# A Fourier layer and a soft mixture of experts on one core: which engine makes two low halves, one fused operation, and two places in the instruction order

## The chip, the cores and the metric

The kernel runs on one NeuronCore of a Trainium2 chip. The metric is the device time of one execution in microseconds, as a median of runs. The core's engines each work through an instruction list of their own in order: TensorE (PE in the profile, its weight loads PEld), VectorE (DVE), ScalarE (ACT), GpSimd (POOL) and SyncE (SP), whose queue issues nearly all DMAs.

## What is computed

The reference has two parts. The first takes x (8 x 2496 x 256), goes to frequencies along the sequence, applies a complex linear layer and a soft threshold, and goes back:

```python
X = np.fft.rfft(x, axis=1)
Yr = Xr @ w_r - Xi @ w_i + b_r
Yi = Xr @ w_i + Xi @ w_r + b_i
Yr = np.sign(Yr) * np.maximum(np.abs(Yr) - lam, 0.0)   # Yi the same
y = np.fft.irfft(Yr + 1j * Yi, n=x.shape[1], axis=1)
```

The second is a soft mixture of 8 experts with 4 slots each on the 19968 tokens of y:

```python
logits = y @ phi                                  # 19968 x 32
d = exp(logits - logits.max(0)); d /= d.sum(0)    # over the tokens
slot_input = d.T @ y                              # 32 x 256
slot_out[e] = relu(slot_input[e] @ w1[e]) @ w2[e]
c = exp(logits - logits.max(1)); c /= c.sum(1)    # over the slots
out = c @ slot_out
```

The inverse transform is linear, so the kernel never forms y: it carries phi, the weights d and the slots through the transforms.

## The kernel before

The 2496 points of a sequence are split as 39 x 64. A batch goes through three kinds of work.

**Steps.** There are 40 steps (`steps`), five per batch, each for four of the 20 frequencies of the 39-point transform. A step has the 64-point transform (`f2`, accumulators px, twice per step), the linear layer (`lin_k`, accumulator pk, 12 matmuls; `lin_y`, accumulators py, 24 matmuls in parts), the threshold (ut, rt), the product with phi (`tp_p`: matmuls pq, ScalarE's copy lg, a transposition of lg, VectorE's p_sb) and, for the last two steps of a batch, transpositions of rt (`tp_t`: accumulator pt, ScalarE's copy T). fp32 operands are split into a high half (rounded) and a low half (what is left), and a product is three matmuls: high, low part of the constant, low part of the operand. xsh and xsl, xh and xl, chpd and clpd are such pairs; xsl, xh and xl and the e = 0 rt are GpSimd's work.

**The 39-point transform** of later batches (`a_group`: xh, xl, accumulator pa, ScalarE's copies ast, written to DRAM and read back as ap).

**Stages of the mixture** (`c_stages`, once for each of batches 0 to 6; the last batch has a function of its own): logits in two transforms with a DRAM passage between (pg, gd, gp, then pL and its copies L), the maximum over the tokens (mx, transposition pm, mall as the running maximum over the batches), the exponentials of L less that maximum (dg, matmul pb, ee), their transforms with a second DRAM passage (pe, ea, ed, eb, then pd and its copies dd) and the sums over the tokens (pr). Beside it runs the softmax over the slots (`c_comb`: cm, cb, cs).

**The order.** Each of these pieces is a generator that yields a plan time; a heap takes the piece with the smallest time, and what it emits is put behind all earlier instructions of its engine. A step lasts 4 units of plan time, a batch 20. So the numbers of `PLAN` are an order written by hand: a number that passes another one moves an instruction in front of another on the same engine and does nothing else. `c_stages` of batch b counts from t0 = 20 b + 26, `tp_p` and `tp_t` of step s from 4 s + 6.

**What the change touches.** `halves` (L747) emits the split and the matmuls of pg, pL, pe and pd, for batches 0 to 5 (batch 6 has `fr` zero and no split). For each of two halves ScalarE copies the high half at `times[0] - 0.9 + 0.4 h`, and 0.3 later the engine that `cl_` names makes the low half (L759); the matmuls of half h come at `times[h]`, ScalarE's copy out of PSUM 0.25 later. For pd (`suni`) the letters are P for the first half and V for the second; the times are 18.1 and 19.05. `c_comb`'s last multiplication cb has the time 17.4 on the same scale. The second pL has 7.95, which is 20 b + 33.95; the px of a step stand at multiples of 4 and 2 units later, among them 20 b + 34. `tp_p` copies lg at 4 s + 7 and `tp_t` copies pt of h = 0 at 4 s + 6.92. L828 to L834 reduce the transposed maxima to `mall[:, b]`, take the maximum with `mall[:, b - 1]`, and scale the identity by it into dg.

Of the kernel before, what the change touches and what calls it, by code (L numbers as in the profile page):

```python
# [11 lines left out]
F32 = mybir.dt.float32  # L12
F32R = mybir.dt.float32r
AF = mybir.ActivationFunctionType
ALU = mybir.AluOpType
# [9 lines left out]
S = 32  # L25
# [54 lines left out]
def _constants():  # L80
# [93 lines left out]
    "sl": 'P',  # L174
    "c0": 0.05,
    "pg": [1.35, 2.3],
    "pL": [7.05, 7.95],
    "pm": 9.05,
    "pb": 10.32,
    "pe": [11.95, 12.98],  # L180
# [18 lines left out]
    "f0": 0.2,  # L199
    "nw": [13, 9],  # L200
    "te": 'A',
    "tp": [0.5, 1.0, 1.9, 1.8],
    "tt": [0.52, 2.505],
    "fr": {'sinv': 1, 'm2': 1, 'f1': 1, 'suni': 1},
    "cl": [0.9, 0.4, 0.3],
    "sc": [10.7, 13.18, 14.7, 17.306],
    "cl_": {'sinv': 'VV', 'm2': 'VV', 'f1': 'VV', 'suni': 'PV'},
    "pda": 1,
    "a1": [-50, -49, -28.95, -28.85, 3.0, 3.684, 6.147, 6.934, 8.231, 8.9, 9.713],
    "e1": [0, 0, 0, 0, 0, 0, 0, 0, 1, 0, 1],  # L210
# [45 lines left out]
def fourier_soft_moe_kernel(ctx: ExitStack, tc: tile.TileContext, t: dict, out: bass.AP):  # L256
# [21 lines left out]
    def wtile(shape, dt, tag, name):  # L278
        if tag in a_bufs:
            return wap.tile(list(shape), dt, tag=tag, name=name, bufs=a_bufs[tag])  # L280
        if tag in main_bufs:
            return wmp.tile(list(shape), dt, tag=tag, name=name, bufs=main_bufs[tag])
        return wcp.tile(list(shape), dt, tag=tag, name=name, bufs=chain_bufs[tag])
# [18 lines left out]
    V, A, P = (_InOrder(tc, e) for e in (nc.vector, nc.scalar, nc.gpsimd))  # L302
# [90 lines left out]
    ident, sgn, suni, sinv, dsc, dmask = (cols[k] for k in ("ident", "sgn", "suni", "sinv", "dsc", "dmask"))  # L393
    f1, m2 = cols["f1"][:P1], cols["m2"][:Q1]
# [11 lines left out]
    mall = cons.tile([128, B], F32, tag="mall", name="mall")  # L406
# [383 lines left out]
    def c_stages(b):  # L790
# [35 lines left out]
        )  # L826
        yield t0 + K_.get("pmr", K_["pm"] + 0.1)
        V.tensor_reduce(out=mall[:, b : b + 1], in_=ps[:, :P1], axis=AX.X, op=ALU.max)  # L828
        if b:
            V.tensor_tensor(  # L830
                out=mall[:, b : b + 1], in0=mall[:, b : b + 1], in1=mall[:, b - 1 : b], op=ALU.max
            )
        dg = wtile([128, S], F32, "dg", f"dg{b}")
        V.tensor_scalar(out=dg, in0=ident[:, :S], scalar1=mall[:, b : b + 1], scalar2=None, op0=ALU.mult)  # L834
        yield t0 + K_["pb"]
        ps = psum(ct_, f"pb{b}")
        mm(out=ps[:P1, :32], lhsT=ones, rhs=dg, start=True, stop=True)
# [3 lines left out]
            out=ee, in0=L[:P1], in1=ps[:P1, :32].unsqueeze(1).broadcast_to([P1, G, S]), op=ALU.subtract  # L841
        )
        if b:
            V.tensor_tensor(
                out=fo[:, b : b + 1], in0=mall[:, b - 1 : b], in1=mall[:, b : b + 1], op=ALU.subtract
# [335 lines left out]
    for b in range(B - 1):  # L1181
        step_to(c_stages(b))
# [248 lines left out]
    for j in range(NBLK):  # L1431
# [4 lines left out]
        for a in range(2):  # L1436
            mm(
                out=pq,
# [73 lines left out]
```

## Time and profile before

| | us |
|---|---|
| median of 3 runs | 552.43 (551.78 to 552.66) |
| the profiled execution | 554.82 |
| its span, first to last instruction | 552.9 |
| TensorE busy in the span | 500.0 (90%) |
| VectorE / ScalarE / GpSimd busy | 371.3 / 320.6 / 263.3 |
| mean granted TensorE clock | 0.954 |

The profile is one execution. A timeline row gives the start in us from the span's start, the duration, the engine, the line, the operation and the tiles as out<-in; a bracket at its end tells how long the engine was idle before it and what ended that. A start can lie some hundredths before the end of the instruction ahead of it on the same engine. Nearly all matmuls carry line 328 and the operations of the other engines line 252, since helpers record them, so the tiles' names tell them apart. The busy share of TensorE is no measure by itself; its waits and its clock say more.

### The profile page before, as it was taken

Reading aid. Unit: us, or ns where it says so; the run is one execution under the profiler, and the core shown is the slowest. Engines: PE = TensorE matmul, PEld = TensorE weight load, DVE = VectorE, ACT = ScalarE, POOL = GpSimd, SP = SyncE. Lnnn points to the kernel's source line nnn. Section 1 sums busy time; section 2 is a strip of 40 time slices with the busy share of each in tenths; the row PEclk is TensorE's granted clock in tenths of the full one; section 3 lists DMA queues with packets and bytes.
Section 4 is the critical chain, followed back from the end, with each engine's and each line's share of the span. In section 5 each row is a group of like instructions: output and inputs, shape, how many; then the busy total and the mean of one; then the engine's idle time right before and its main releaser. Section 6 shows DMA issues by size and latency. Waiting matters only on the chain.

```text
span 552.9 us, 11988 instructions
## 1 busy us (share of the span) xinstructions
PE 500.0 (90%) x4438; PEld 407.7 (74%) x4438; DVE 371.3 (67%) x718; ACT 320.6 (58%) x736; POOL 263.3 (48%) x277
## 2 busy tenths in 40 slices
PE   8879999997999979996999699969998999999991
PEld 5579778885787768785778678858887886558881
DVE  3347876788479836984688567865886477526771
ACT  4357567675566646673657466755565555427771
POOL 0028576667456655565565565662334432233310
PEclk9979999999799979997999799988998999999997
DMA  8988788688656866757485957673659799638998
GB/s 303 315 254 309 240 243 239 188 281 213 200 150 219 221 206 169 239 165 225 129 278 173 247 148 257 195 192 103 173 188 242 178 368 393 221 132 335 406 405 337
DMA packets 90461, 131.04 MB, mean 237 GB/s; under 512 B 40204, under 2 KB 61836, under 8 KB 90404
## 3 DMA queue, kind: packets, MB, share of 16 engines
q1 hardware_dynamic: 89460, 128.16, 72.5%
q10 hardware_dynamic: 944, 2.13, 1.2%
q8 instruction: 35, 0.57, 0.4%
q14 instruction: 22, 0.18, 0.1%
HBM read 69.25 MB, written 50.00 MB: 216 GB/s over the span
## 4 chain that ended last, share of the span: by engine, by line
PE 65%; DVE 10%; DMA 7%; POOL 7%; ACT 5%; issue 4%; SPq 1%; ACTq 0%; POOLq 0%; DVEq 0%
PE py L328 15%; PE pq L328 9%; PE pk L328 9%; PE pa L328 8%; PE px L328 8%; PE pt L703 3%; PE pr L328 3%; DVE mx L252 2%; POOL rt L252 2%; DMA gd<-g_sb 2%; PE pc L703 2%; PE pe L328 2%; DMA xr<-in_x 1%; PE pd L328 1%; POOL xsl L252 1%
## 5 line engine op out<-in xcount | busy, mean ns | idle before, releaser
L252 POOL TENSOR_TENSOR xsl<-xsm,xsh 128x256 fp32r<-128x256 f32 x77 | 65.5, 851 | 154.1 <-ACT xsh L252 139.5
L328 PEld LDWEIGHTS px<-smov,ap 128*128 128x128 f32 x640 | 79.5, 194 | 17.6 <-issue 5.7
L252 DVE SCALAR_TENSOR_TENSOR ut<-py,pk,k 128x256 f32<-128x256 f32 x160 | 69.8, 477 | 33.7 <-PE py L328 32.5
L328 PE MATMUL px<-smov,ap 128*128 128x128 f32 x640 | 86.9, 280 | 1.2 <-ACT ast L252 1.2
L252 DVE TENSOR_TENSOR xsm<-px,xsm 128x256 f32<-128x256 f32 x80 | 33.1, 414 | 57.9 <-ACT xth L252 28.1
L252 ACT COPY ast<-pa 128x512 f32<-128x512 f32 (+1 forms) x88 | 45.2, 558 | 27.9 <-PE pa L328 27.8
L252 DVE TENSOR_TENSOR xtl<-px,xth 128x512 fp32r<-128x512 f32 x80 | 54.3, 679 | 0.1
L328 PE MATMUL py<-xth,nwsh 128*128 128x256 f32 (+1 forms) x160 | 53.9, 337 | 0.0
L328 PE MATMUL pk<-xsh,w_rh 128*128 128x256 f32 (+1 forms) x160 | 50.6, 316 | 0.0
L252 ACT CAST xth<-px 128x512 fp32r<-128x512 f32 x80 | 47.1, 591 | 5.1 <-PE py L328 4.2
L252 POOL TENSOR_TENSOR rt<-ut,rt 128x512 f32<-128x512 f32 x36 | 50.0, 1389 | 0.1
L328 PE MATMUL pk<-xsl,w_rh 128*128 128x256 f32 (+1 forms) x160 | 48.2, 301 | 0.0
L328 PE MATMUL pk<-xsh,w_rl 128*128 128x256 f32 (+1 forms) x160 | 48.0, 300 | 0.0
L328 PE MATMUL py<-xth,wdh 128*128 128x256 f32 (+1 forms) x160 | 45.8, 286 | 0.0
L328 PE MATMUL py<-xtl,nwsh 128*128 128x256 f32 (+1 forms) x160 | 45.5, 284 | 0.0
L328 PE MATMUL py<-xth,nwsl 128*128 128x256 f32 (+1 forms) x160 | 45.4, 284 | 0.0
L328 PE MATMUL py<-xth,wdl 128*128 128x256 f32 (+1 forms) x160 | 45.3, 283 | 0.0
L328 PE MATMUL py<-xtl,wdh 128*128 128x256 f32 (+1 forms) x160 | 45.2, 283 | 0.0
L252 ACT COPY xsm<-px 128x256 f32<-128x256 f32 x80 | 30.0, 375 | 26.0 <-PE px L328 25.0
L252 POOL TENSOR_TENSOR xh<-xr 128x512 f32<-128x512 f32 (+1 forms) x36 | 44.2, 1227 | 0.0
L328 PE MATMUL pq<-rhs,ct 128*128 128x512 f32 x156 | 41.7, 405 | 0.2
L252 ACT CAST xsh<-xsm 128x256 fp32r<-128x256 f32 x80 | 33.1, 414 | 12.1 <-DVE xsm L252 11.7
(230 smaller groups left out, 1312.2 us busy)
## 6 DMA issues: line engine op xcount, KB each, us to landing
ap<-adr SPq DMA_DIRECT2D x76, 256.0 KB
out<-ost SPq DMA_DIRECT2D x37, 512.0 KB
xr<-in_x SPq DMA_DIRECT2D x35, 512.0 KB
adr<-ast SPq DMA_DIRECT2D x20, 768.0 KB
y<-z SPq DMA_DIRECT2D x112, 96.0 KB
w<-in_moe_w SPq DMA_DIRECT2D x21, 512.0 KB
adr<-ast SPq DMA_DIRECT2D x7, 512.0 KB
w<-in_moe_w SPq DMA_DIRECT2D x14, 256.0 KB
```

The lines of the kernel that those rows point to most:

```text
L252: return lambda *a, **k: self.tc.keep_in_program_order(f(*a, **k))
L328: tc.keep_in_program_order(nc.tensor.matmul(**kw))
L703: tc.keep_in_program_order(nc.tensor.transpose(out=out, in_=in_, identity=identity))
```

## The change

Four edits:

- `cl_`, `suni`: 'PV' becomes 'VP'. The first low half of pd's operand is made by VectorE, the second by GpSimd. It applies to batches 0 to 5.
- dg is made in one operation, (mall[b] max mall[b - 1]) times the identity, straight from the reduction; mall[b] itself gets the maximum behind it. Batches 0 to 6 (in batch 0 the second value is the first again).
- The second pL of batches 0 to 5 has the time 8.02 in place of 7.95, so that its matmuls stand behind the px at 34 + 20 b, and its copy and what follows it get 0.07 more.
- lg has the time 4 s + 6.9 in place of 4 s + 7: it stands ahead of the copy of pt at 4 s + 6.92.

```diff
@@ PLAN
-    "pL": [7.05, 7.95],
+    "pL": [7.05, 8.02],
-    "tp": [0.5, 1.0, 1.9, 1.8],
+    "tp": [0.5, 0.9, 1.9, 1.8],
-    "cl_": {'sinv': 'VV', 'm2': 'VV', 'f1': 'VV', 'suni': 'PV'},
+    "cl_": {'sinv': 'VV', 'm2': 'VV', 'f1': 'VV', 'suni': 'VP'},
@@ c_stages
         V.tensor_reduce(out=mall[:, b : b + 1], in_=ps[:, :P1], axis=AX.X, op=ALU.max)
+        dg = wtile([128, S], F32, "dg", f"dg{b}")
+        V.scalar_tensor_tensor(
+            out=dg, in0=mall[:, b : b + 1].broadcast_to([128, S]), scalar=mall[:, max(b - 1, 0) : max(b, 1)],
+            in1=ident[:, :S], op0=ALU.max, op1=ALU.mult,
+        )
         if b:
             V.tensor_tensor(
                 out=mall[:, b : b + 1], in0=mall[:, b : b + 1], in1=mall[:, b - 1 : b], op=ALU.max
             )
-        dg = wtile([128, S], F32, "dg", f"dg{b}")
-        V.tensor_scalar(out=dg, in0=ident[:, :S], scalar1=mall[:, b : b + 1], scalar2=None, op0=ALU.mult)
         yield t0 + K_["pb"]
```

## Rows read from the trace of the kernel before

**Rows 1.** The page, its chain that ended last, shares by engine.
```profile
PE 65%; DVE 10%; DMA 7%; POOL 7%; ACT 5%; issue 4%; SPq 1%; ACTq 0%; POOLq 0%; DVEq 0%
```
**Rows 2.** TensorE's waits: us in total, times, longest.
```profile
PE pd L328 <- POOL clpd L252: 24.2, 6, 4.4
PE pb L328 <- DVE dg L252: 5.6, 5, 1.2
PE pq L703 <- ACT lg L252: 2.5, 9, 0.7
```
**Rows 3.** Timeline around pd of batch 1, GpSimd and TensorE.
```profile
191.82 1.91 POOL L252 TENSOR_TENSOR rt<-ut,rt 128x512 f32<-128x512 f32 x1
...
194.62 1.26 POOL L252 TENSOR_TENSOR xl<-xr 128x512 f32<-128x512 f32 x1
195.84 0.85 POOL L252 TENSOR_TENSOR clpd<-eb,chpd 128x320 fp32r<-128x320 f32 x1
196.75 0.63 PE L328 MATMUL pd<-clpd,sunih 128*128 128x320 f32 x1 [4.43 <-POOL clpd L252]
```
**Rows 4.** Timeline of the same stretch, VectorE.
```profile
191.45 1.16 DVE L252 TENSOR_TENSOR cb<-cb,cs 128x704 f32<-128x704 f32 x1
192.53 1.55 DVE L252 TENSOR_TENSOR clpd<-eb,chpd 128x320 fp32r<-128x320 f32 x1
```
**Rows 5.** Timeline around pd of batch 5, VectorE and TensorE.
```profile
421.37 1.35 DVE L252 TENSOR_TENSOR clpd<-eb,chpd 128x320 fp32r<-128x320 f32 x1
...
423.49 0.42 PE L328 MATMUL pd<-clpd,sunih 128*128 128x320 f32 x1 [2.08 <-POOL clpd L252]
```
**Rows 6.** Stretches: length, busy of PE, PEld, DVE, ACT, POOL; clock, DMA, GB/s.
```profile
138.83:143.90 5.07, 5.07 (x23) 5.07 (x24) 1.96 (x4) 2.79 (x7) 0.73 (x1) 0.50 0.82 223
143.90:195.00 51.10, 47.08 (x463) 38.52 (x461) 39.97 (x75) 32.12 (x76) 31.68 (x32) 1.00 0.67 197
...
419.00:423.50 4.50, 2.06 (x15) 1.42 (x13) 3.50 (x6) 1.50 (x5) 3.67 (x3) 1.00 0.92 285
423.50:427.20 3.70, 3.70 (x18) 3.70 (x19) 1.62 (x3) 1.81 (x4) 0.73 (x1) 0.54 1.01 293
```
**Rows 7.** The chain that ended last, in order of time: start, us, what.
```profile
139.47 2.56 PE pk L328 x12
...
142.88 1.93 PE py L328 x12
...
151.75 0.89 PE px L328 x8
...
153.09 1.42 PE pk L328 x12
154.51 1.41 PE py L328 x12
```
**Rows 8.** By tile, clpg and dg: ns min/median/max, first and last start.
```profile
L252 DVE TENSOR_TENSOR clpg<-p_sb,chpg x12: 479/483/694, 93.2 to 381.9; 128x320 fp32r<-128x320 f32 x12
L252 DVE SCALAR_TENSOR_TENSOR dg<-mall,pk x1: 252/252/252, 469.0 to 469.0; 128x32 f32<-128x32 f32 x1
```
**Rows 9.** Timeline around dg of batch 1.
```profile
170.87 0.73 POOL L252 TENSOR_TENSOR xsl<-xsm,xsh 128x256 fp32r<-128x256 f32 x1 [1.97 <-PE pq L703]
171.17 0.45 DVE L252 TENSOR_TENSOR mall<-mall 128x1 f32<-128x1 f32 x1
171.56 1.26 POOL L252 TENSOR_TENSOR rt<-ut,rt 128x512 f32<-128x512 f32 x1
...
171.65 1.21 DVE L252 TENSOR_SCALAR dg<-pk,mall 128x32 f32<-128x32 f32 x1
...
172.78 0.86 DVE L252 SCALAR_TENSOR_TENSOR ut<-py,pk,k 128x256 f32<-128x256 f32 x2
172.91 0.39 PE L328 MATMUL pb<-dg,ones 128*117 128x32 f32 x2 [1.16 <-DVE dg L252]
...
176.44 0.53 DVE L252 TENSOR_TENSOR clpe<-ee,chpe 117x352 fp32r<-117x352 f32 x1 [0.21 <-ACT chpe L252]
```

## The prediction

> **What bounds the kernel now.** I read the page's chain first: of the work that ended last, TensorE is 65% [rows 1]. So the end moves only where TensorE waits or runs slowly, and the second view is the list of TensorE's waits [rows 2]. It is short: 24.2 us in six waits of the matmul group pd for its low half from GpSimd, 5.6 us in five waits of pb for dg, 2.5 us in nine waits of a transposition for lg. Each of these is touched by the change.
>
> The third view is the timeline around one pd, that of batch 1. TensorE's first pd group (high, low constant, low operand) stands still for 4.43 us until 196.75, so since 192.32 [rows 3]. What it waits for, GpSimd's clpd, runs at 195.84. It isn't late because its operand is: it stands in GpSimd's order behind rt, xh and xl, which ends only at 195.88 [rows 3]. VectorE made the other low half, of which pd needs only later, already from 192.53 on for 1.55 us [rows 4]. The wait is 4.43 us in batches 0 to 4 and 2.08 us in batch 5 [rows 2, 5].
>
> The fourth view is the granted clock. From 138.83, when the pd of batch 0 is released, to 143.90 it is 0.50, which is 1.2 GHz; from there to 195 it is 1.00, which is 2.4 GHz [rows 6]. So behind such a wait TensorE does its work at half speed: twelve pk matmuls take 2.56 us there and 1.42 us later, twelve py matmuls 1.93 and 1.41 [rows 7]. The 2.08 us wait of batch 5 has the same tail: 0.54 over 3.70 us [rows 6].
>
> **The change part by part. Low halves of pd.** The operation for the first half leaves GpSimd and goes to VectorE at plan time 17.5, that for the second goes to GpSimd at 17.9. On VectorE the multiplication cb (17.4) stands just ahead, p_sb behind. So the new operation stands where the old one stood in batch 1: directly behind cb, at 192.53 [rows 4]. What is it worth there? Alone, a subtraction of this size takes VectorE 0.483 us (clpg) [rows 8]; here it took 1.55 us. The rows say why: GpSimd's rt started at 191.82, while cb ran, took 1.91 us until 193.73, and the subtraction ended 0.35 us after it [rows 3, 4]. VectorE and GpSimd took turns: cb, rt, subtraction, in the order in which they came. I take the same end, 194.08, since neither the neighbours nor the place differ. TensorE then goes on at about 194.12 and waits 1.8 us in place of 4.43: 2.63 us less, five times, 13.1 us. In batch 5 VectorE's operation ran from 421.37 for 1.35 us, to 422.72, and pd was released at 423.49 [rows 5]: 0.7 us. Sum 13.9 us. The bounds: if VectorE gets no wait behind cb, the operation ends at 193.01 and the wait is 0.7 us, 3.7 us saved per batch; if it had to let xh and xl pass too, it would end 0.35 us behind 195.88, at 196.23, and 0.5 us is saved.
>
> The Trainium skill, "GPSIMD Engine Reference", section "4.1 Engine selection", would have such an operation on VectorE, since GpSimd is about twice as slow with two inputs. By that alone the first half would cost 0.48 us and the sum would be the upper bound, 19 us. The trace agrees when VectorE is alone (0.48 against 0.85 us) and not here, beside rt: 1.55 us [rows 3, 4, 8].
>
> What queues behind? On VectorE p_sb, which is needed only for the next pg, and after it work for a px that TensorE has only just made. On GpSimd the low half keeps its place behind xl and is for the second pd group. TensorE reaches that group after pk, transpositions and py: 194.12 plus 1.42 and 1.41 us is 196.95 [rows 7], and the transpositions come on top; GpSimd is done at 196.69 [rows 3]. So its wait is covered by 0.3 us and more; a longer GpSimd queue would show there.
>
> **The clock.** Per batch the half speed costs 1.14 us in pk and 0.52 in py [rows 7], 1.66 us; and since 5.07 us passed at half speed [rows 6] it can't be more than 2.5. I take 2.1, for the transpositions and the pd matmul between, five times 10.5. In batch 5 it is 3.70 times 0.46, 1.7 us [rows 6]. Together 12.2 us, if the clock doesn't fall. No row shows a wait of 1.8 us. Waits of 1.16 us left the clock at 1.00 (that of pb lies within the stretch from 143.90) [rows 6, 9]; one of 2.08 us didn't. So both ends, nothing and 12.2, are open. By distance 1.8 is nearer to 2.08; but the 2.08 us wait began at 421.41 and the stretch up to 423.5 still shows the clock at 1.00 [rows 6], so the fall came no sooner than some 2 us after the idling began, and a wait of 1.8 us is over by then, one of 1.35 all the more. I take the 12.2 us as regained and give the fall a large chance.
>
> **dg and the running maximum.** Removed from dg's path: the maximum (0.45 us) and the scaling (1.21 us); added: one operation that does both [rows 9]. In the last batch that very form took 0.252 us [rows 8]. It would be issued at 171.17, beside xsl, which GpSimd holds until 171.60, and be done by 171.75 instead of 172.86: pb's wait of 1.16 us goes. But what is next? The maximum itself now comes third, when rt (from 171.56, 1.26 us) already runs; dg took 1.21 us because it fell on rt, and the maximum will in its place [rows 9]. So VectorE's two ut begin no sooner than the 172.78 of today, rather 0.15 us later. py's accumulator is freed by them, and clpe (176.44), for which the third pe matmul would have to wait next, hangs on the VectorE chain behind them [rows 9]. TensorE gains 1.1 us at pb and gives it back at py and pe. I cost it at nothing; the bounds are 5.6 us gained [rows 2] and the 0.15 us lost per batch, 0.9 us.
>
> **Second pL behind px.** The matmuls stay, the eight px (0.89 us [rows 7]) go first. L's second copy comes up to 0.9 us later, which ScalarE's work on pa hides by half; with it the reduction mx, the head of the VectorE chain to dg. It takes from pb what dg's part gave. Between 0 and 0.45 us lost in each of six batches; I take 0.2, 1.2 us, since px and its ScalarE copies come earlier in exchange.
>
> **lg ahead of pt's copy.** It moves a copy that ScalarE could have made while it waited for pt. It removes the waits for lg where a pt stands beside: I take 1.1 of the 2.5 us [rows 2]; bounds 0 and 2.5. pt's copy isn't needed until pr, several us later. It also lets xsh and xsl start a little earlier; I count nothing for that.
>
> **Sum.** 13.9 + 12.2 + 0 - 1.2 + 1.1 = 26.0 us. The profiled execution took 554.82 us (span 552.9), 2.4 us over the median of 552.43; the differences hold for both, and I take them from the median: 526 us.
>
> **The rivals.** (1) The clock falls behind the shortened waits as well. For: 2.08 us was enough. Then 12.2 us of the sum is missing: 538 us, or some way between if it falls only in some batches (532 for half). Chance 0.25. (2) VectorE goes on straight behind cb and the operation takes 0.48 us: 5 times 1.1 us more, 520 us; against it speaks that the same two neighbours did take turns in batch 1. With dg's full 5.6 us it would be 515. Chance 0.10. (This is the case of the page named above.) (3) The change doesn't do what it says: VectorE's first half is held until GpSimd's queue is empty. Then five waits shrink by 0.5 us, 2.5 in all, the clock falls as before, and the time is about 550 us. Chance 0.03. (4) Slower: the VectorE chain from L's copy over mx, the held maximum and ut to ee and clpe becomes what TensorE waits for, 0.9 us of px plus 0.15 us in six batches, at most 6.3 us. It decides the sign once the pd part brings less than that, so only where the first half is held as in case 3: 552.4 - 2.5 + 6.3 is 556 us. Against it: none of these is a wait of TensorE's today. Chance 0.03. The forecast, 520 to 530 us by the bounds of the smaller parts, has the remaining 0.59.
>
> **Range and chances.** 516 to 539 us: from case 2 with half of dg's bound to the clock's full fall; it leaves out cases 3 and 4 and the far ends of the others. A measurement of this kernel can tell about 0.2% (1.1 us) from no change. Faster: 0.59 + 0.25 + 0.10, and a part of case 3, 0.95; same 0.02; slower 0.03.
>
> **What would show it.** In the profile after: pd's waits are for VectorE and some 1.8 us long, six in all, about 10 us; VectorE's clpd still takes 1.3 to 1.6 us; GpSimd's clpd ends before the second pd group; the granted clock is 1.00 right behind pd, and pk takes 1.4 us there; pb's waits are gone or small, and VectorE's maximum takes about 1.2 us in dg's place, with new waits of py for ut or of pe for clpe; waits for lg have halved. The prediction is wrong if the clock still falls behind pd, if the second pd group waits for GpSimd, or if a transfer (eb ahead of pd) is late once the batches are shorter.

## The result, and the profile after

The changed kernel takes 534.8 us (median of 4 runs, 533.44 to 537.2), the kernel before 552.28 us beside it (4 runs); the ratio is 0.969 with a 95% interval of 0.965 to 0.973. That is 17.5 us less, where 26 had been forecast: the time lies inside the range of 516 to 539 and 8.8 us above the predicted 526. The profiled execution took 533.44 us (span 531.7) beside the 554.82 (552.9) of before, and its mean granted clock is 0.972 where it was 0.954.

TensorE's waits after the change (us in total, times, longest), against [rows 2]:

```profile
PE pd L328 <- DVE clpd L252: 12.3, 6, 2.1
PE pb L328 <- DVE dg L252: 2.9, 6, 0.6
...
PE pe L328 <- ACT chpe L252: 1.0, 1, 1.0
PE py L328 <- DVE ut L252: 1.0, 5, 0.2
PE pq L703 <- ACT lg L252: 0.7, 1, 0.7
```

pd's six waits have halved, from 24.2 to 12.3 us, and VectorE now ends them instead of GpSimd. pb's went from 5.6 to 2.9 us, lg's from 2.5 to 0.7. Two small ones are new, py for ut and pe for chpe, 2.0 us together (before, pe waited for chpe for 0.2 us). Waits of pa early in the kernel differ from one execution to the next (for xr 0.4 us before and 2.0 after, for xh 2.1 before and none after) and are left aside here.

The timeline around pd of batch 1 answers to [rows 3, 4]:

```profile
183.83 0.88 DVE L252 SCALAR_TENSOR_TENSOR ut<-py,pk,k 128x256 f32<-128x256 f32 x2 [0.30 <-PE py L328]
184.62 1.00 DVE L252 TENSOR_TENSOR cb<-cb,cs 128x704 f32<-128x704 f32 x1
184.82 1.91 POOL L252 TENSOR_TENSOR rt<-ut,rt 128x512 f32<-128x512 f32 x1
185.54 1.54 DVE L252 TENSOR_TENSOR clpd<-eb,chpd 128x320 fp32r<-128x320 f32 x1
187.14 0.41 PE L328 MATMUL pd<-clpd,sunih 128*128 128x320 f32 x1 [2.05 <-DVE clpd L252]
188.88 0.87 POOL L252 TENSOR_TENSOR clpd<-eb,chpd 128x320 fp32r<-128x320 f32 x1
```

The order is the forecast one: cb, rt, subtraction. rt starts while cb runs and ends at 186.73; VectorE's subtraction, in line from 185.54, ends 0.35 us behind it, exactly the distance that [rows 3, 4] show. It takes 1.54 us, and TensorE waits 2.05 us, not 1.8. GpSimd's half ends at 189.75, and no second pd group waits for it.

The stretches around that pd (length, busy of PE, PEld, DVE, ACT, POOL; clock, DMA share, GB/s), against [rows 6]; the first is the one behind batch 0's pd, the second the wait itself:

```profile
134.20:140.00 5.80, 5.80 (x46) 4.80 (x47) 3.39 (x7) 4.24 (x10) 5.34 (x7) 1.00 0.88 248
185.08:187.14 2.06, 0.01 (x2) 0.01 (x1) 2.06 (x3) 0.00 (x0) 2.06 (x2) 1.00 0.90 304
187.14:187.58 0.44, 0.44 (x3) 0.44 (x4) 0.14 (x1) 0.00 (x0) 0.44 (x1) 1.00 0.94 214
187.58:190.99 3.41, 3.41 (x18) 3.41 (x17) 1.77 (x4) 1.92 (x5) 2.85 (x4) 0.50 1.01 291
```

Here the forecast's missing part is seen. Behind batch 0's wait the clock stays at 1.00, 2.4 GHz. Behind batch 1's it stays there for 0.44 us after TensorE has been released, and then falls to 0.50, 1.2 GHz, for 3.41 us. So it goes in five of the six batches, 0.44 to 0.66 us after the release. Before, it was at 0.50 for some 6.8 us around the end of each of the five long waits (it fell while they still ran, as in this stretch of batch 0's wait) and for 3.4 us behind batch 5's.

```profile
137.00:138.83 1.83, 0.00 (x0) 0.00 (x0) 0.00 (x0) 0.00 (x0) 1.78 (x2) 0.51 0.93 259
```

Around dg of batch 1, against [rows 9]:

```profile
164.52 0.72 POOL L252 TENSOR_TENSOR xsl<-xsm,xsh 128x256 fp32r<-128x256 f32 x1 [2.50 <-ACT xsh L252]
164.82 0.47 DVE L252 SCALAR_TENSOR_TENSOR dg<-mall,pk 128x32 f32<-128x32 f32 x1
165.20 1.27 POOL L252 TENSOR_TENSOR rt<-ut,rt 128x512 f32<-128x512 f32 x1
165.33 1.16 DVE L252 TENSOR_TENSOR mall<-mall 128x1 f32<-128x1 f32 x1
165.35 0.39 PE L328 MATMUL pb<-dg,ones 128*117 128x32 f32 x2 [0.49 <-DVE dg L252]
166.41 0.86 DVE L252 SCALAR_TENSOR_TENSOR ut<-py,pk,k 128x256 f32<-128x256 f32 x2
167.43 0.36 PE L328 MATMUL py<-xth,nwsh 128*128 128x256 f32 x1 [0.19 <-DVE ut L252]
```

dg ends at xsl's end and releases pb after 0.49 us. The maximum of one column, which pb does not need (the difference fo behind pb and the next batch's dg are the first to read it), now stands beside rt, takes 1.16 us and holds ut; py waits for ut in turn. The whole stall moved from dg to the maximum, as forecast.

### The profile page after: what moved, and what is told of

It is laid out like the page before. It is cut to its first block, busy times and chain, and to the rows that moved or that the text cites. A ratio compares the mean times of both kernels' runs of the same rounds, so it can differ in the third digit from the quotient of the medians.

```text
span 531.7 us, 11986 instructions
## 1 busy us (share of the span) xinstructions
PE 494.4 (93%) x4438; PEld 399.9 (75%) x4438; DVE 371.0 (70%) x718; ACT 321.1 (60%) x736; POOL 265.3 (50%) x277
## 5 line engine op out<-in xcount | busy, mean ns | idle before, releaser
L252 POOL TENSOR_TENSOR xsl<-xsm,xsh 128x256 fp32r<-128x256 f32 x77 | 66.9, 870 | 143.0 <-ACT xsh L252 142.6
L328 PEld LDWEIGHTS px<-smov,ap 128*128 128x128 f32 x640 | 78.3, 192 | 21.6 <-issue 7.6
L328 PE MATMUL pk<-xsh,w_rh 128*128 128x256 f32 (+1 forms) x160 | 49.0, 306 | 0.0
L328 PE MATMUL pk<-xsh,w_rl 128*128 128x256 f32 (+1 forms) x160 | 46.8, 292 | 0.0
```

Of the source, the lines that this page charges most:

```text
L252: return lambda *a, **k: self.tc.keep_in_program_order(f(*a, **k))
L328: tc.keep_in_program_order(nc.tensor.matmul(**kw))
```

## Experiments

What was open was twofold: whether the gain comes from the swapped halves at all, and whether the missing 9 us are the clock's falls or sizes of other terms. The runs come in three groups; those of one group share a chip and the runs of the kernel before, and each ratio is against those.

### The change again, and its parts

> The changed kernel as it is, beside the kernels of the next three runs on one chip. Every theory: 533 to 537 us, pd waits for VectorE some 2.05 us in six batches (12.3 us), and the clock falls behind most of them for 3.4 us.

The same kernel on another chip: 532.59 us (531.85 to 533.77) against 552.59, ratio 0.965 (0.961 to 0.969). The waits of pd are the same, 12.3 us in six, but the clock fell behind four of them. Three stretches (columns as above) show a fall that comes late, and none behind a wait of nearly the same length (2.00 us):

```profile
244.82:246.30 1.48, 1.48 (x12) 1.48 (x13) 0.14 (x1) 1.03 (x3) 1.48 (x2) 1.00 1.02 316
246.33:249.74 3.41, 3.41 (x18) 3.41 (x17) 2.45 (x4) 2.12 (x5) 2.37 (x4) 0.50 0.88 262
299.35:304.00 4.65, 4.65 (x40) 4.08 (x40) 3.06 (x7) 3.61 (x8) 4.19 (x5) 1.00 1.02 306
```

pd of batch 2 was released at 244.82; TensorE worked at full speed for 1.5 us, and only then the clock fell. Batch 3's wait (297.35 to 299.35) left it at 1.00, and so did the 2.05 us of batch 4. This execution also prices a fall by itself: from pb to pb a batch takes 54.55 us with one (168.46 to 223.02, 223.02 to 277.55) and 53.05 without (277.55 to 330.60), so a fall costs 1.5 us.

The swap alone, on the kernel before:

```diff
-    "cl_": {'sinv': 'VV', 'm2': 'VV', 'f1': 'VV', 'suni': 'PV'},
+    "cl_": {'sinv': 'VV', 'm2': 'VV', 'f1': 'VV', 'suni': 'VP'},
```

> The kernel before with one edit alone: the first low half of pd's operand by VectorE, the second by GpSimd. Theory A (the gain is pd's shorter wait and the shorter fall of the clock behind it): pd waits about 1.8 us per batch, 1.35 in batch 5, and the time is 535 to 539 us, over three quarters of the gain. Rival B (the four edits only work together; alone the swap brings half or less): 543 us or more.

535.26 us (535.02 to 535.84), ratio 0.970 (0.966 to 0.974): nearly all of the gain. Its waits, the timeline of batch 1, and the stretches of pd's wait and behind it:

```profile
PE pd L328 <- DVE clpd L252: 10.9, 6, 1.8
PE pb L328 <- DVE dg L252: 5.8, 5, 1.2
```

```profile
185.19 0.88 DVE L252 SCALAR_TENSOR_TENSOR ut<-py,pk,k 128x256 f32<-128x256 f32 x2 [0.22 <-PE py L328]
...
186.36 1.91 POOL L252 TENSOR_TENSOR rt<-ut,rt 128x512 f32<-128x512 f32 x1
...
188.66 0.63 PE L328 MATMUL pd<-clpd,sunih 128*128 128x320 f32 x1 [1.81 <-DVE clpd L252]
```

```profile
186.86:188.66 1.80, 0.00 (x0) 0.00 (x0) 1.80 (x3) 0.00 (x0) 1.80 (x2) 0.98 1.03 323
188.66:192.00 3.34, 3.33 (x15) 3.34 (x16) 1.19 (x4) 1.80 (x4) 3.29 (x4) 0.50 1.05 303
```

The wait is 1.81 us in each of the six batches, the predicted 1.8 to a hundredth; and behind every one of them the clock is at 0.50 for 3.4 us. Here the fall came as the wait ended or up to 0.2 us ahead of that (the 0.98 over batch 1's wait), so 1.6 to 1.8 us after TensorE had come to a stand. So the forecast's wait was right, and its claim that a wait of 1.8 us leaves the clock alone was wrong without any other edit in play. It also tells why the wait is 2.05 us in the whole change. Here TensorE comes to a stand at 186.85, 1.66 us behind the start of ut, and rt ends 3.08 us behind it; in the whole change these are 1.25 us (185.08 less 183.83) and 2.90 us. TensorE comes 0.4 us earlier, the operand 0.2. Of the three other edits lg's move is the one that stands there: with lg back behind pt's copy (below), pd's waits are shorter by 0.25 us each.

The other edits without the swap:

> The changed kernel with the swap undone, so dg's fused operation, the second pL behind px and lg ahead of pt's copy alone. Theory A: pd waits for GpSimd 4.4 to 4.7 us as before and the clock falls for 6.8 us behind it; pb's waits shrink to 0.5 us, and what they lose comes back at py, pe and pd; 549 to 552 us. Rival B: the three bring 6 us or more by themselves: 546 us or less.

551.21 us (549.0 to 554.84), ratio 0.999 (0.995 to 1.002). dg, the second pL and lg bring nothing that can be told from no change while pd waits for GpSimd:

```profile
PE pd L328 <- POOL clpd L252: 25.7, 6, 4.7
PE pb L328 <- DVE dg L252: 2.9, 6, 0.5
...
PE pe L328 <- ACT chpe L252: 1.0, 1, 1.0
PE py L328 <- DVE ut L252: 1.0, 5, 0.2
...
PE pq L703 <- ACT lg L252: 0.7, 1, 0.7
```

The rows balance: 2.7 us less at pb and 1.8 less at lg, 1.5 more at pd (TensorE is there earlier, GpSimd isn't) and 1.8 more at pe and py, together 1.2 us; measured were 1.4, which the runs' interval does not tell from nothing.

### Is it the clock? Filling the wait

Here TensorE is given work in the wait: matmuls of the identity into an unused tile, ahead of pd's third matmul, whose result nobody reads. They add work and take nothing out. The first try used 15:

```diff
+                    if n == "suni" and h == 0 and i == 2:
+                        idle = psum("ps", f"idle{out[0]}")
+                        for _ in range(15 if out[0] == "pd5" else 15):
+                            mm(out=idle[:, :128], lhsT=ident, rhs=ident, start=True, stop=True, skip_group_check=True)
```

> The changed kernel with 15 matmuls of 128 columns on the identity (results unused) in front of the third matmul of the first pd group in batches 0 to 5; by the spacing of px they take about 1.7 us, less than the wait of 2.05. Theory C (the clock falls because TensorE idles in that wait): pd is released at the same time, the clock stays at 1.00 behind it, pk takes 1.42 us there, and 5 times some 1.7 us are saved: 525 to 529 us. Rival D (the fall has another cause, or the extra matmuls delay pd by as much): the fall stays, 533 us or more.

533.48 us (531.46 to 535.72), ratio 0.967 (0.961 to 0.972), no faster than the change itself, and mis-sized. Batch 1 shows it:

```profile
184.16 3.51 PE L328 MATMUL idlepd<-pk 128*128 128x128 f32 x30
184.78 1.55 DVE L252 TENSOR_TENSOR clpd<-eb,chpd 128x320 fp32r<-128x320 f32 x1
```

Each of the 15 is two records, and 3.51 us is 0.234 each, twice what I had taken. The operand was there at 186.33, and pd's third matmul started at 187.43, behind the fill, 1.1 us later. The clock fell behind no pd, but that gain was spent. So once more, with 7:

> The changed kernel with 7 extra matmuls on the identity ahead of the third matmul of the first pd group. In the run with 15 of them one took 0.234 us, all 3.5 us, 1.2 us longer than the wait that they were to fill; 7 take 1.64 us of the 2.05. Theory C (the clock falls because TensorE idles there, and a fall costs the 1.5 us by which the batch periods of the changed kernel with and without a fall differ, 54.55 and 53.05 us): no fall behind pd, pd released when VectorE is ready, 526 to 528 us. Rival D (the regained clock is lost again to other engines): 531 us or more.

525.5 us (524.56 to 526.53) against 551.25, ratio 0.953 (0.950 to 0.957). Batch 1, and the stretch behind it:

```profile
185.16 1.72 PE L328 MATMUL idlepd<-pk 128*128 128x128 f32 x14
185.77 1.55 DVE L252 TENSOR_TENSOR clpd<-eb,chpd 128x320 fp32r<-128x320 f32 x1
...
187.38 0.42 PE L328 MATMUL pd<-clpd,sunih 128*128 128x320 f32 x1 [0.50 <-DVE clpd L252]
```

```profile
187.38:191.00 3.62, 3.62 (x30) 3.62 (x31) 1.68 (x4) 3.12 (x7) 3.31 (x4) 1.00 1.03 276
```

pd is released no earlier than it was (the subtraction is the same), the clock stays at 1.00 behind all six, and the period from pb to pb is 53.0 us instead of 54.5. By the ratios that is 6.5 to 8.6 us less than the change itself (0.965 and 0.969 on its two chips); five falls at 1.5 us are 7.5. So work that is of no use, put into a wait, gives back what the falls cost, and with that the main part of what was missing is shown to be the clock, not a term of another edit. That the time is also the 526 us of the forecast is in part chance, since other terms were off in both directions (below).

The same on the kernel before, 16 extra matmuls in batches 0 to 4 and 7 in batch 5:

> The kernel before with 16 extra matmuls (3.7 us) in pd's wait of 4.43 us in batches 0 to 4 and 7 (1.6 us) in that of 2.08 us in batch 5. The wait for GpSimd's low half stays, only the clock shouldn't fall. Theory C: period 58.0 less about 2.2 us, 540 to 542 us. Rival D: 548 us or more.

542.14 us (540.81 to 546.38), ratio 0.985 (0.980 to 0.990). The stretch behind pd of batch 1 is at full clock:

```profile
193.30:198.00 4.70, 4.70 (x40) 4.05 (x40) 2.89 (x6) 3.62 (x8) 1.50 (x3) 1.00 0.85 233
```

A batch takes 55.7 us in place of 58.03, so the 6.8 us at half speed had cost 2.3 us; 2.1 was taken in the prediction. The size of that term was nearly right; what was wrong is how much of it the change gives back. The whole run gained 9.1 us and not the 13 that five such tails and batch 5's would give back: in its profiled execution, the slowest of the four, pL waits 4.0 us (0.8 before), and behind one of these waits the clock falls.

### Out of the turn: the subtraction ahead of cb

The second rival said that the operation would take 0.48 us if VectorE went straight on. That can be had by letting cb stand behind it:

```diff
-        s_ = steps or [PLAN["cm"] + d for d in (0, 0.5, 1.3, 2.3, 3.1, 3.8)]
+        s_ = steps or [PLAN["cm"] + d for d in (0, 0.5, 1.3, 2.3, 3.25, 3.8)]
```

> The changed kernel with cb's plan offset 3.25 in place of 3.1, so that VectorE makes pd's first low half ahead of cb. Theory E (what is left of pd's wait is cb and GpSimd's rt, which take turns with VectorE): clpd takes at most 0.8 us, pd's first wait falls from 2.05 to 0.3 us or less, the clock stays, and the second pd group waits up to 0.6 us for GpSimd's half, which is now next: 516 to 522 us. Rival F (VectorE's subtraction is slow by itself, or rt is let in ahead of it anyway): clpd still takes 1.5 us, 530 us or more.

527.55 us (525.13 to 528.52), ratio 0.956 (0.952 to 0.961), above the 516 to 522 that I had expected. Batch 1:

```profile
186.17 0.59 DVE L252 TENSOR_TENSOR clpd<-eb,chpd 128x320 fp32r<-128x320 f32 x1
186.38 1.53 POOL L252 TENSOR_TENSOR rt<-ut,rt 128x512 f32<-128x512 f32 x1
186.69 1.97 DVE L252 TENSOR_TENSOR cb<-cb,cs 128x704 f32<-128x704 f32 x1
186.82 0.42 PE L328 MATMUL pd<-clpd,sunih 128*128 128x320 f32 x1 [0.18 <-DVE clpd L252]
```

```profile
PE pd L328 <- POOL clpd L252: 5.1, 5, 1.0
PE pL L328 <- DMA gp<-gd: 3.1, 1, 3.1
```

Now the subtraction takes 0.59 us and TensorE waits 0.18. cb pays, with 1.97 us beside rt. The period of a batch falls from 54.5 to 52.4 us, and no clock falls behind pd. Two new waits take part of it: the second half from GpSimd, whose instruction now takes 1.3 us and comes late for the second pd group (five times 1.0), and one wait of 3.1 us for a transfer, the pL of the last stage, behind which the clock fell once (0.66 over the next 5 us).

Both halves on VectorE, cb still behind:

```diff
-    "cl_": {'sinv': 'VV', 'm2': 'VV', 'f1': 'VV', 'suni': 'VP'},
+    "cl_": {'sinv': 'VV', 'm2': 'VV', 'f1': 'VV', 'suni': 'VV'},
```

> As the run with cb behind the first low half, and the second low half by VectorE too, behind cb. Theory E: no wait of the first group, and none of the second for GpSimd: 514 to 519 us, at least 1 us less than with GpSimd's second half. Rival G (GpSimd's second half was never late, and VectorE pays for the extra operation): the same as that run or up to 3 us more.

523.25 us (522.41 to 524.3), ratio 0.949 (0.946 to 0.953), again above what was expected (514 to 519). The second group's wait for GpSimd is gone, and the wait of pL stays; px now waits for VectorE instead:

```profile
PE px L328 <- DVE xtl L252: 4.0, 4, 2.3
```

The longest of these, 2.30 us, left the clock alone (the wait, then what follows):

```profile
303.44:305.74 2.30, 0.00 (x1) 0.04 (x1) 2.30 (x6) 0.71 (x2) 0.23 (x1) 1.00 0.63 100
305.74:312.00 6.26, 6.26 (x72) 5.58 (x73) 4.20 (x10) 4.10 (x12) 5.13 (x6) 1.00 0.64 215
```

It is longer than the 1.81 us of the swap alone, which was followed by a fall six times of six. So the length of a wait doesn't settle by itself whether the clock falls.

### The small edits, with the clock held

With the 7 extra matmuls in place each small edit can be weighed without a fall behind pd (the kernel before takes 552.37 us beside these). Early in the kernel one fall of 3.4 us remains in the profiled executions of the first two runs below (18.5 us from the start), and none in those of the third or of the seven matmuls above. Each ratio stands against the 0.953 (0.950 to 0.957) of the seven matmuls above, which ran on another chip; all three intervals overlap with it, so the times alone settle none of the three, and the waits carry what is said. The second pL back ahead of px:

```diff
-    "pL": [7.05, 8.02],
+    "pL": [7.05, 7.95],
```

> The changed kernel with the 7 extra matmuls in pd's wait (no fall of the clock, 525.5 us) and the second pL back ahead of px. My step says that pL behind px costs 0.2 us a batch, since L's second copy and mx come later (ScalarE idles 0.48 and VectorE 0.64 us there): without it mx starts some 0.6 us earlier, pb waits 0.3 us less or not at all, and the time is 523 to 525.5 us. Rival (px and its copies earlier are worth more): 526.5 us or more, with waits of pL for L's first copy.

523.41 us (522.34 to 525.36), ratio 0.948 (0.944 to 0.951). pb's waits, 2.9 us with the edit, are gone altogether. So behind px the second pL takes back half of dg's gain at pb, 2.9 of 5.6 us. By times it costs 2.1 us, by the ratios 3, if these differences are more than noise.

lg back behind pt's copy:

```diff
-    "tp": [0.5, 0.9, 1.9, 1.8],
+    "tp": [0.5, 1.0, 1.9, 1.8],
```

> The same with lg back behind pt's copy. My step says 1.1 us of waits for lg are saved by the change. If they are a gain of the whole, this run takes 526 to 527.5 us; if they were given back in pd's wait (TensorE comes to pd earlier, VectorE's half not), pd's wait shrinks by 0.2 us here and the time stays within 0.5 us of 525.5.

528.24 us (526.67 to 528.98), ratio 0.956 (0.953 to 0.960), above both of the expected times.

```profile
PE pq L703 <- ACT lg L252: 2.4, 9, 0.7
...
PE pd L328 <- DVE clpd L252: 1.5, 6, 0.3
```

lg's waits are back at 2.4 us in nine. pd's six waits, 3.0 us in the run with all edits, are 1.5. The move is worth 2.7 us by times, 1.5 by the ratios.

The running maximum out of ut's way, to where it is first needed:

```diff
-        if b:
-            V.tensor_tensor(
-                out=mall[:, b : b + 1], in0=mall[:, b : b + 1], in1=mall[:, b - 1 : b], op=ALU.max
-            )
         yield t0 + K_["pb"]
...
         if b:
+            V.tensor_tensor(
+                out=mall[:, b : b + 1], in0=mall[:, b : b + 1], in1=mall[:, b - 1 : b], op=ALU.max
+            )
             V.tensor_tensor(
                 out=fo[:, b : b + 1], in0=mall[:, b - 1 : b], in1=mall[:, b : b + 1], op=ALU.subtract
```

> The same with the running maximum taken behind ee, just ahead of fo, so that it doesn't stand between dg and ut. My step says that it takes dg's place beside GpSimd's rt and holds ut by 1.1 us: now ut starts right behind dg, py's waits for ut (5 of 0.2 us) and pe's for chpe (1.0 us in one batch) go, ee and clpe come about 1 us earlier, and the time is 522.5 to 525 us. Rival (the hold is covered by other work): 525.5 us as before.

523.32 us (521.47 to 526.01), ratio 0.947 (0.944 to 0.951). The waits of py for ut are gone, pe's for chpe is back at 0.2 us, pb's stay at 2.9 us. So they did hang on the held maximum.

### What the pieces make together

cb behind, both halves on VectorE, the maximum behind ee, and no extra matmuls:

> VectorE makes both low halves of pd, the first ahead of cb, and the running maximum stands behind ee: what the runs point to, without extra matmuls. The sum of the two: 523.3 less 1 to 3 us, 520 to 522.5 us; 523 us or more if the hold of ut is covered.

516.41 us (516.11 to 518.85), ratio 0.936 (0.932 to 0.939), the fastest of all and below the expected 520 to 522.5. Its waits, and the stretch that follows the first pd group of batch 1:

```profile
PE px L328 <- DVE xtl L252: 3.2, 4, 1.5
PE pL L328 <- DMA gp<-gd: 3.0, 1, 3.0
```

```profile
184.00:192.00 8.00, 8.00 (x94) 6.32 (x93) 6.97 (x13) 6.22 (x16) 8.00 (x8) 1.00 0.89 232
```

TensorE waits 0.18 us at pd and then works on without a pause at full clock. The late maximum lowers the ratio by 0.014 here, 7.6 us, and by 0.006 in the run before. Part of the 7.6 may be the clock: in the profiled execution of both halves on VectorE it fell twice, early in the kernel and behind the 3.1 us wait of pL, and here it stood at 1.00 from 5.5 to 507 us, behind the 3.0 us wait of pL too. At 1.5 us a fall that would be 3 us, which wasn't tried by itself.

## Why the prediction was right where it was, and where it failed

**pd's wait: right.** The taking of turns, the place in the order and the end 0.35 us behind rt were as worked out from [rows 3, 4]; 1.81 us in the swap alone, against 1.8. In batch 5 I had taken VectorE's start of before, 1.35 us; there it was 1.81 as everywhere. In the whole change the wait is 2.05 us, since TensorE comes 0.4 us earlier behind ut and the operand only 0.2. Saved: 24.2 less 12.3, 11.9 us, of the 13.9 forecast. The second rival (no wait behind cb) did not come; with the subtraction ahead of cb, and so ahead of rt, it did.

The Trainium skill, "SBUF — State Buffer", section "SBUF: two separate sides", says that a VectorE instruction with two inputs in SBUF and a GpSimd one that reads SBUF lock each other out, for a whole instruction, in the order in which they start. The trace agrees: the same subtraction takes 1.54 us behind rt and 0.59 us ahead of it, and then cb takes 1.97 us in place of 1.00.

**The clock: the step that failed.** All 12.2 us were taken as regained, because [rows 6] show the clock still at 1.00 when batch 5's 2.08 us wait ended: "the fall came no sooner than some 2 us after the idling began, and a wait of 1.8 us is over by then". The row was read rightly; the conclusion didn't follow, at two points. It took the delay of one wait for the least that there is: in the swap alone the fall came 1.6 to 1.8 us after the idling began, six times of six. And it assumed that a fall that hasn't come when the wait ends won't come. It does: 0.44 to 0.66 us after the release in the change, 1.0 to 1.5 us after it in the repeat. That row itself had the fall behind the wait, at 0.54 from 423.50 on. By distance to the nearest row, which I had set aside, 1.8 us belonged to 2.08. What the shorter wait did change is the length of the tail, 3.4 us for 6.8.

The term, measured: 2.3 us per long wait before, five times, and 1.5 for batch 5's is 13.0 us; after, five falls at 1.5 are 7.5. Regained are 5.5 us of the 12.2. This is the first rival, part way, whose 532 us for half a regain stands 3 us from the measured 534.8 and at that of the repeat. The time lies inside the range because the range took in this rival's price, not because the forecast's own path held.

**dg: right, with a different split.** pb's waits shrank by 2.7 us, and 1.8 us came back at pe and py, where it was expected. The new waits are the held maximum's, as its own run shows.

**Second pL: a cost, as taken; 1.2 us was probably too small.** It is seen at pb, whose remaining 2.9 us are gone without it, and by times it is 2.1 us, though the intervals overlap. In the sum below it is already inside pb's balance.

**lg: undersized, 1.1 taken and 1.8 us of waits gone;** but pd's waits are longer with it.

By the measured terms, 11.9 + 5.5 + 0.9 + 1.8 makes 20.1 us. These rows are read from the two profiled executions, which differ by 21.4 us. The medians differ by 17.5, with an interval of 15.0 to 19.4, so the sum lies a little outside it, and by 20.0 on the chip of the repeat. What makes up the 2.6 us on the first chip isn't shown.

**GpSimd's second half** was in time, as argued, and in the change itself pd waited for clpd alone, so the transfer eb was not late. Two others were waited for there, ap for 0.8 and gp for 0.3 us, and gp for up to 3.1 us once the batches became shorter still.

Two numbers of the record are off without bearing on this. Case 2 with half of dg's bound comes to 518 us, not the 516 at which the range begins. And the measurement's interval was 2.2 us to either side, twice the 1.1 that was taken.

## What to carry to other kernels

A wait that is cut is not yet worth its clock: whether TensorE's clock falls behind a shorter wait must be bounded by the nearest wait in the trace that did show a fall, and a fall can come after the wait is over. Where a wait can't be removed, a little unused TensorE work in it can be worth more than it costs, if it ends before the operand comes. And where VectorE and GpSimd take turns, the order of arrival decides who pays: put the operation that TensorE waits for ahead of its neighbour, and one that nobody waits for behind it.

## What the runs showed of the hardware

- In the changed kernel and its repeat the clock fell 0.44 to 1.5 us after an idle stretch of TensorE was over, and stood at 1.2 GHz for 3.41 us then. Such a tail cost 1.5 us.
- Waits of 1.81 us came with a fall six times of six, waits of about 2.05 us five times of six in one run and four in another; one of 2.30 us and one of 3.0 us were not followed by any, while those of 3.1 us in two other runs were. What tells these apart stays open.
- The maximum of one column takes 1.17 us beside GpSimd's rt (batches 1 to 5) and 0.16 us in the last two batches, where GpSimd has nothing beside it. By tile, the changed kernel's (ns min/median/max, first and last start):

```profile
L252 DVE TENSOR_TENSOR mall<-mall x7: 159/1167/1174, 165.3 to 447.8; 128x1 f32<-128x1 f32 x7
```
- Fifteen 128x128 fp32 matmuls of the identity took 3.51 us, 0.234 each, in two records apiece.
